# Starting the instruction streams of four engines at multiples of 128 slots in a one-token attention and MLP kernel

## The chip, the cores and the metric

The kernel runs on one core of one Trainium2 chip. The metric is the device time of one execution in microseconds (us); lower is better. Quoted times are medians of several executions. Beside them stands the span of one profiled execution, from its first to its last recorded instruction. The span is about 1.8 us shorter than the time of the same execution (659.0 and 660.86 us for the kernel before).

## The reference

Two sequences, one new token each, 32 heads of 128, a cache of 8192 positions, then a gated MLP. All inputs are bf16.

```python
def _A_ref(x, k_cache, v_cache, wq, wo):          # x: (2, 1, 512); caches: (2, 32, 8192, 128)
    q = (x @ wq).reshape(B, Sq, Hq, Dh).transpose(0, 2, 1, 3)
    scores = jnp.einsum("bhqd,bhkd->bhqk", q, k) * (Dh ** -0.5)
    p = _softmax(scores, axis=-1)
    o = jnp.einsum("bhqk,bhkd->bhqd", p, v)
    return o.transpose(0, 2, 1, 3).reshape(B, Sq, Hq * Dh) @ wo
# ... _B_ref: relu(x @ W_gate) * (x @ W_up) @ W_down
h = x + _A_ref(_layernorm(x), A_k_cache, A_v_cache, A_wq, A_wo)
h2 = h + _B_ref(_layernorm(h), B_W_gate, B_W_up, B_W_down)
```

The two caches are 268 MB of the 281.13 MB that the profile counts, so nearly all the traffic is one pass over K and V.

## The kernel before

The 64 pairs of sequence and head are worked off in 16 groups of four heads. One group is 8.4 MB of K and 8.4 MB of V. VectorE multiplies K by the query and adds up by halves, ScalarE takes exponentials, and TensorE multiplies by V. SyncE issues the loads. GpSimd builds constants in the first 8 us and is idle from then until about 634 us.

The kernel writes its own instruction lists, one for each engine, and emits them at the end (cut):

```python
class Streams:
    ...
    def emit(self, eng, engine):
        for waits, fn, gives in self.lists[eng]:
            for name, value in waits:
                engine.wait_ge(self.sem(name), value)
            if fn is not None:
                last = fn()
                if gives is not None and last is not None:
                    last.then_inc(self.sem(gives[0]), gives[1])
```

The first entries are these (cut). On ScalarE and SyncE the first entries are loads:

```python
    s.op("pool", lambda: pool.memset(eps_t, EPS), writes=["eps"])
    # ... mean_c, ident
    s.op("pool", lambda: pool.affine_select(out=ident, ...), reads=["ident"], writes=["ident"])
    s.op("pool", lambda: pool.memset(row_of, 0.0), writes=["row_of"])
    # ...
    s.dma("act", "dx", lambda: act.dma_start(out=x_row, ...), writes=["x_row"])
    s.dma("sp", "dwq", lambda: sync.dma_start(out=wq_v, ...), writes=["va", "vb", "vc"])
    load_k(0, 0, T // 2)
    load_k(0, T // 2, T)
    load_k(1)
    # ... from here on the layer norm, the query, the loop
    for n in range(L):                       # L = 15 of the 16 groups
        # ...
        scores(n, HALVES if n == 0 else (0, T))   # VectorE, then ScalarE
        if n + 2 < N:
            load_k(n + 2)
        # ...
```

The softmax here doesn't subtract the row's maximum and nothing guards it: scores larger than these inputs give would overflow.

Of the kernel before, what the change touches and what calls it, by code (L numbers as in the profile page):

```python
# [17 lines left out]
class Streams:  # L18
# [65 lines left out]
    def dma(self, eng, name, fn, reads=(), writes=(), extra=()):  # L84
        return self.op(eng, fn, reads, writes, extra, (name, 16), (name, 16))

    def wait(self, eng, tokens):
        self.lists[eng].append((self.needs(eng, (), (), tokens), None, None))

# [3 lines that stand above are left out]
                engine.wait_ge(self.sem(name), value)  # L93
            if fn is not None:
                last = fn()
                if gives is not None and last is not None:
                    last.then_inc(self.sem(gives[0]), gives[1])


# [1 line left out]
def kernel(  # L101
# [109 lines left out]
    s = Streams(nc, ("pe", "dve", "act", "pool", "sp"))  # L211
    for name in ("v_in", "p_in", "o_in"):
        s.sem(name)
    pe, dve, act, pool, sync = nc.tensor, nc.vector, nc.scalar, nc.gpsimd, nc.sync



    s.op("pool", lambda: pool.memset(eps_t, EPS), writes=["eps"])
    s.op("pool", lambda: pool.memset(mean_c, 1.0 / D), writes=["mean"])
    s.op("pool", lambda: pool.memset(ident, 0.0), writes=["ident"])  # L220
    s.op("pool", lambda: pool.affine_select(
        out=ident, in_=ident, compare_op=ALU.not_equal, fill=1.0, base=0, pattern=[[-1, P]],
        channel_multiplier=1), reads=["ident"], writes=["ident"])
    s.op("pool", lambda: pool.memset(row_of, 0.0), writes=["row_of"])
    s.op("pool", lambda: pool.memset(zm, 0.0), writes=["zm"])
    s.op("pool", lambda: pool.memset(pm, 0.0), writes=["pm"])
# [28 lines left out]
    def rows_of(cache, n):  # L255
        b, i = divmod(n, NQ)
        return cache[b, G * i:G * i + G].rearrange("h s d -> (h s) d").rearrange(
            "(p t) d -> p t d", p=P)
# [3 lines left out]
    def parts(lo, hi):  # L262
        cuts = [c for c in KEYS if lo <= c < hi]
        return [KEYS[c] for c in cuts]

    def load_k(n, lo=0, hi=T):
        t = kt[n % 2]
        keys = [f"k{n % 2}{x}" for x in parts(lo, hi)]
        s.dma("sp", f"dk{n}_{lo}", lambda: sync.dma_start(
            out=t[:, lo:hi, :], in_=rows_of(A_k_cache, n)[:, lo:hi, :]), writes=keys)  # L270
# [14 lines left out]
    load_k(0, 0, T // 2)  # L285
    load_k(0, T // 2, T)
    load_k(1)



# [484 lines left out]
```

## Time and profile before

| kernel before | value |
|---|---|
| time, median of 3 | 661.48 us (661.25 to 661.62) |
| span of the profiled execution | 659.0 us |
| start of the first product with K | 22.86 us |
| last landing of a load | 654.82 us |

The page of the kernel before follows, cut to the head, the rows of VectorE (DVE) and DMA in its 40 slices, and the queues. In the slices a 9 means busy for 90% or more of the slice. A queue line has packets, MB and share of the time of 16 transfer engines.

```profile
span 659.0 us, 3129 instructions
...
DVE  1799999999999999999999999999999999999962
...
DMA  9999999999999999999999999999999999999996
...
q1 hardware_dynamic: 6648, 281.06, 98.9%
q8 instruction: 3, 0.05, 0.0%
q14 instruction: 2, 0.02, 0.0%
```

The transfers are busy throughout (q1 for 98.9% of the span), and VectorE nearly so (617.2 us, 94%). The lines of kind "instruction" I take for the engines' own programs arriving: fifteen jumps to a new block, added on one engine, raised the packets on q14 from two to 16 (`act_15`) and 17 (`pool_15`, both below). By the trace's records each packet on q8 is 16 KB, and each on q14 is 8 KB.

The table of stretches of the kernel before has these columns: stretch, its length, busy us and instruction count of each engine, granted TensorE clock, DMA share, GB/s.

```profile
22.90:401.00 378.10, 53.44 (x600) 22.39 (x600) 375.88 (x86) 27.76 (x75) 0.00 (x0) 0.56 1.00 434
401.00:595.00 194.00, 29.63 (x328) 12.30 (x328) 190.39 (x44) 15.94 (x44) 0.00 (x0) 0.57 1.00 433
```

VectorE is busy for 375.88 of 378.10 us in the first stretch. In the second it leaves 3.6 us idle while the transfers stay at 1.00.

The timeline of the kernel before shows three products with K in that second stretch. Its columns are start, length, engine, line, operation, and in brackets the idle time of the engine and what ended it.

```profile
440.45 17.22 DVE L374 TENSOR_TENSOR k<-k,qrep 128x32768 bf16<-128x32768 bf16 x1 [0.42 <-DMA k<-in_A_k_cache_dram]
479.15 17.23 DVE L374 TENSOR_TENSOR k<-k,qrep 128x32768 bf16<-128x32768 bf16 x1 [0.72 <-DMA k<-in_A_k_cache_dram]
517.86 17.23 DVE L374 TENSOR_TENSOR k<-k,qrep 128x32768 bf16<-128x32768 bf16 x1 [0.72 <-DMA k<-in_A_k_cache_dram]
```

Each waits for its K load, and the period is 38.7 us. Before 400 us the period is 37.9 us, which is what VectorE needs for one group. So VectorE sets the pace first and the transfers set it later.

The beginning and the end come from the chain of work that ended last (start, length, what):

```profile
1.43 21.41 DMA k<-in_A_k_cache_dram
...
22.86 8.70 DVE k L374
...
641.94 12.88 DMA k<-in_B_W_down_dram
654.82 0.14 issue
654.95 0.42 PE y L667 x16
655.37 0.03 issue
655.40 0.29 DVE sc L731
```

The K load that lands at 22.83 us starts VectorE. The last W_down load, landing at 654.82 us, starts the last matmuls. Store and closing barrier follow, 4.2 us from that landing to the end of the span.

### The profile page before, as it was taken

Reading aid. Unit: us, or ns where it says so; the run is one execution under the profiler, and the core shown is the slowest. Engines: PE = TensorE matmul, PEld = TensorE weight load, DVE = VectorE, ACT = ScalarE, POOL = GpSimd, SP = SyncE. Lnnn points to the kernel's source line nnn. Section 1 sums busy time; section 2 is a strip of 40 time slices with the busy share of each in tenths; the row PEclk is TensorE's granted clock in tenths of the full one; section 3 lists DMA queues with packets and bytes.
Section 4 is the critical chain, followed back from the end, with each engine's and each line's share of the span. In section 5 each row is a group of like instructions: output and inputs, shape, how many; then the busy total and the mean of one; then the engine's idle time right before and its main releaser. Section 6 shows DMA issues by size and latency. Waiting matters only on the chain.

```text
span 659.0 us, 3129 instructions
## 1 busy us (share of the span) xinstructions
PE 114.0 (17%) x1244; PEld 47.1 (7%) x1244; DVE 617.2 (94%) x180; ACT 59.4 (9%) x155; POOL 7.7 (1%) x29
## 2 busy tenths in 40 slices
PE   2100302103030110303012030300203030030364
PEld 1000100001010000101000010100101010010112
DVE  1799999999999999999999999999999999999962
ACT  2301010010101001010100101010010101001100
POOL 3000000000000000000000000000000000000010
PEclk9755655657555575755557575555757555575776
DMA  9999999999999999999999999999999999999996
GB/s 382 443 445 434 398 442 445 445 434 398 442 445 442 442 398 442 442 445 438 430 410 442 445 442 434 402 445 442 442 442 402 438 442 442 442 426 414 432 411 244
DMA packets 6669, 281.13 MB, mean 427 GB/s; under 512 B 812, under 2 KB 816, under 8 KB 1544
## 3 DMA queue, kind: packets, MB, share of 16 engines
q1 hardware_dynamic: 6648, 281.06, 98.9%
q8 instruction: 3, 0.05, 0.0%
q14 instruction: 2, 0.02, 0.0%
q10 hardware_dynamic: 16, 0.01, 0.0%
HBM read 281.06 MB, written 0.00 MB: 426 GB/s over the span
## 4 chain that ended last, share of the span: by engine, by line
DVE 74%; DMA 24%; SPq 1%; issue 1%; PE 0%
DVE k L374 34%; DVE k L380 33%; DMA k<-in_A_k_cache_dram 22%; DVE sc L229 5%; DMA k<-in_B_W_down_dram 2%; SPq L549 1%; DVE osb L463 1%; DVE om L459 1%; SPq L540 0%; PE y L667 0%; SPq L283 0%; DVE ou L229 0%; DVE sc L731 0%; DVE rep L475 0%; SPq L770 0%
## 5 line engine op out<-in xcount | busy, mean ns | idle before, releaser
L374 DVE TENSOR_TENSOR k<-k,qrep 128x32768 bf16<-128x32768 bf16 (+3 forms) x18 | 275.9, 15327 | 4.9 <-DMA k<-in_A_k_cache_dram 4.9
L380 DVE TENSOR_TENSOR k<-k 128x4096 bf16<-128x4096 bf16 (+6 forms) x72 | 267.4, 3713 | 2.5
L416 PE MATMUL o<-v,pm 128*32 128x512 bf16 x960 | 85.8, 536 | 465.6 <-PEq L444 465.6
L393 ACT ACTIVATE pm<-sc 32x256 bf16<-32x256 f32 (+2 forms) x68 | 48.2, 709 | 563.1 <-DVE sc L229 562.3
L416 PEld LDWEIGHTS o<-v,pm 128*32 128x32 bf16 x960 | 36.1, 129 | 514.9 <-issue 508.6
L229 DVE TENSOR_REDUCE sc<-k 128x256 f32<-128x2048 bf16 (+2 forms) x17 | 36.7, 2161 | 0.6
L463 DVE TENSOR_REDUCE osb<-om 128x128 f32<-128x512 f32 x16 | 16.5, 1030 | 0.6
L393 ACT ACTIVATION_READ_ACCUMULATOR pm<-sc 32x1 f32 x68 | 15.8, 233 | 0.0
L359 DVE CAST qrep<-mm 32x512 bf16<-32x512 f32 x4 | 2.8, 695 | 11.5 <-PE mm L343 11.5
L459 DVE TENSOR_TENSOR om<-o,turn_of 128x512 f32<-128x512 f32 x16 | 10.9, 682 | 1.4 <-PE o L416 1.4
L423 PE MATMUL rep<-osb,spread 128*32 128x128 f32 x40 | 3.2, 363 | 47.7 <-DVE osb L463 44.5
L416 PE MATMUL o<-k,pm 128*32 128x512 bf16 x64 | 6.8, 583 | 8.7 <-ACT pm L393 5.8
L356 ACT ACTIVATE qrep<-mm 32x512 bf16<-32x512 f32 x12 | 7.0, 586 | 8.8 <-PE mm L343 8.5
L532 POOL TENSOR_TENSOR zm<-zm,zx 128x1 f32<-128x1 f32 x1 | 0.2, 190 | 626.2 <-ACT pm L393 626.2
L343 PE MATMUL mm<-v,om 128*64 128x512 bf16 x32 | 5.8, 512 | 9.3 <-DMA v<-in_A_wq_dram 8.4
L633 DVE STREAM_TRANSPOSE osb<-mm 128x512 f32<-128x512 f32 x1 | 0.7, 717 | 5.6 <-PE mm L617 5.6
L423 PEld LDWEIGHTS rep<-osb,spread 128*32 128x32 f32 x40 | 1.2, 127 | 50.0 <-DVE osb L463 46.1
L617 PE MATMUL mm<-v 128*2 128x512 bf16 x32 | 4.1, 609 | 0.9 <-DMA v<-in_A_wo_dram 0.8
L343 PEld LDWEIGHTS mm<-v,om 128*64 128x64 bf16 x32 | 2.3, 141 | 12.4 <-issue 9.7
L416 PEld LDWEIGHTS o<-k,pm 128*32 128x32 bf16 x64 | 2.0, 134 | 13.4 <-ACT pm L393 7.2
L731 DVE CAST sc<-y 128x128 bf16<-128x128 f32 x1 | 0.3, 291 | 2.7 <-PE y L667 2.7
L311 DVE COPY xc<-st 128x8 f32<-128x8 f32 x1 | 0.2, 166 | 2.7 <-PE st L304 2.7
(82 smaller groups left out, 35.1 us busy)
## 6 DMA issues: line engine op xcount, KB each, us to landing
k<-in_A_k_cache_dram SPq DMA_DIRECT2D x2, 4096.0 KB, 26.8
v<-in_A_wq_dram SPq DMA_DIRECT2D x1, 4096.0 KB, 12.2
k<-in_A_v_cache_dram SPq DMA_DIRECT2D x1, 4096.0 KB, 31.4
k<-in_A_v_cache_dram SPq DMA_DIRECT2D x1, 3072.0 KB, 38.3
v<-in_A_wo_dram SPq DMA_DIRECT2D x1, 2048.0 KB, 18.9
k<-in_B_W_gate_dram SPq DMA_DIRECT2D x1, 1376.0 KB, 14.8
k<-in_B_W_up_dram SPq DMA_DIRECT2D x1, 1032.0 KB, 17.0
k<-in_A_v_cache_dram SPq DMA_DIRECT2D x1, 1024.0 KB, 40.3
```

The costliest lines, as they stand in the source:

```text
L229: s.op("dve", lambda: dve.tensor_reduce(out=out_, in_=in_, axis=axis, op=ALU.add), reads=reads, writes=writes)
L343: last = pe.matmul(out=ps[h * B * Q:(h + 1) * B * Q], lhsT=xnb[:, c].rearrange("p b q -> p (b q)"), rhs=wq_h[:, c, g:g + QP, h0 + h, :], s ...
L356: s.op("act", lambda src=src, dst=dst: act.activation(out=dst, in_=src, func=ACT.Copy), reads=[f"mm{t}"], writes=[key])
L374: s.op("dve", lambda: dve.tensor_tensor(out=kp, in0=kp, in1=_view(qrep[:, b, i, :], 0, [[0, hi - lo], [1, Dh]]), op=ALU.mult), reads=keys ...
L380: s.op("dve", lambda half=half, width=width: dve.tensor_tensor(out=kp[:, :, 0:half], in0=kp[:, :, 0:half], in1=kp[:, :, half:width], op=AL ...
L393: last = act.activation(out=p_of[ps, lo // TG:hi // TG, :, h], in_=sc2[n % 2][ps, lo:hi].rearrange("p (g t) -> p g t", t=TG), func=ACT.Exp ...
L416: last = pe.matmul(out=o[g:g + W2], lhsT=pm[:, t // TG, :], rhs=vs[:, t:t + TG, :].rearrange("p t d -> p (t d)"), start=(t < P // Q * TG), ...
L423: return pe.matmul(out=rep_ps[u * Q:(u + 1) * Q, :], lhsT=spread.rearrange("k h m -> k (h m)"), rhs=osb[:, u, :], start=True, stop=True, s ...
L459: s.op("dve", lambda: dve.tensor_tensor(out=om.rearrange("p (t d) -> p t d", d=Dh), in0=o.rearrange("p (t d) -> p t d", d=Dh), in1=_view(t ...
L463: fn = lambda: dve.tensor_reduce(out=osb[:, u, :], in_=om.rearrange("p (t d) -> p d t", d=Dh), axis=AXIS.X, op=ALU.add)
L549: s.dma("sp", "d" + key, lambda: sync.dma_start(out=wd_sb[rows, f0:f0 + FT, :].rearrange("p j n -> p (j n)"), in_=wd_in[q0:min(q1, NM):row ...
L617: last = pe.matmul(out=ar_ps[g:g + B], lhsT=oc[:, k, :], rhs=wo_sb[:, k, :], start=False, stop=(k + P // Q >= NK), skip_group_check=True)
```

## The change

The intent, as I read it, is that an engine should not cross from one block of its program to the next at an awkward place. By a block I mean what one 8 KB instruction packet brings; that a multiple of 128 slots is the edge of one was not measured. The directive `addr_align(128, ...)`, put behind each engine's first instructions, asks that the stream go on at the next multiple of 128 instruction slots. The trace of after shows one branch more on each of the four engines (3133 instructions instead of 3129): VectorE's at 0.97 us, ahead of its first instruction, ScalarE's at 1.51 us, after its first load, GpSimd's at 1.66 us, after building the identity, and SyncE's at 2.94 us, after its four first loads. TensorE is left as it is.

```diff
+    def new_block(self, eng, engine):
+
+        self.lists[eng].append(((), lambda: engine.addr_align(128, offset=0, max_nops=0), None))
+
@@ emit
-                if gives is not None and last is not None:
+                if gives is not None:
@@
+    s.new_block("dve", dve)
     s.op("pool", lambda: pool.memset(eps_t, EPS), writes=["eps"])
@@
         channel_multiplier=1), reads=["ident"], writes=["ident"])
+    s.new_block("pool", pool)
@@
     load_k(1)
+    s.new_block("sp", sync)
+    s.new_block("act", act)
```

The changed line in `emit` drops a test and adds no work. The diff adds 8 lines ahead of the loop, so L374 is L382.

## The prediction

Three passages are cut out of the recorded text where it is marked, since no trace or run of this case shows them: a statement on how instructions are fetched, an estimated cost of a jump whose target had not been fetched yet, and a count of where the second crossings lie. 661.2 us is the 661.48 us of before less a gain of about 0.3 us ("part of a microsecond"), with the branches off the critical path. "The shared queue" is q14 of the page.

> **What bounds the kernel now.** The data transfers, with VectorE close behind. 281 MB move at a mean of 427 GB/s over a 659.0 us span (page). In the stage table the stretch 22.9 to 401 us has DMA share 1.00 with VectorE busy 375.9 of 378.1 us; 401 to 595 us has DMA share 1.00 with VectorE busy 190.4 of 194.0 us. The period of a head group in the timeline is 37.9 us early and 38.7 us late, where VectorE waits for K loads. VectorE's start is set by the K landing at 22.83 us, the end by the last W_down landing at 654.8 us, then 4.2 us of matmul, copy, store and closing barrier.
>
> **What the change does.** The instruction order shows one extra directive on each of four engines and nothing moved. Each takes one branch over padding, so the rest of its stream starts at a multiple of 128 slots. This can only buy better placed crossings from one instruction block to the next. [...]
>
> **Gains and costs.** Inside the span of before there are two 8 KB instruction packets, at 177.2 and 201.3 us, 0.31 us each; one more starts at 659.4 us, behind the last instruction. Around 177 and 201 us there is no gap: VectorE goes on within 0.03 us, ScalarE had nothing to do. Near the likely second crossings[...] no gap lacks a semaphore that explains it. So the gain is at most part of a microsecond, in or behind the closing barrier.
>
> Cost: about 0.15 us a branch (those at 0.8 us)[...]. All jumps are early and off the critical path: SyncE's comes after its four loads are issued (2.9 us), its next issue at 20.05 us; VectorE waits for TensorE until 2.65 us; GpSimd's results are due at about 23 us. The normalised x is ready at 5.9 us, its consumer waits for wq until 13.25 us: 7 us of slack. The K landing at 22.8 us stays.
>
> **Predicted time: 661.2 us, range 659.8 to 662.6.** Chances: faster by over 2% 0.01, within 2% 0.98, slower by over 2% 0.01.
>
> **What would show it.** Right: first K product at 22.8 to 22.9 us; SyncE's first issues unchanged; the shared queue's instruction packets within the first few us instead of at 177 and 201, without a gap; periods 37.9 then 38.7 us; last landing within 0.5 us of 654.8. Wrong: a gap of 1 to 3 us in VectorE or SyncE without a semaphore to explain it, the first product after 23.5 us, or a tail off 4.2 us by over 0.5 us.
>
> **What would make it wrong.** A crossing in the tail of before whose fetch waits behind the data; a target that isn't fetched ahead; or a fetch block other than I think, so that the new layout crosses in the tail where the old one didn't.

## The result, and the profile after

| | before | after |
|---|---|---|
| time, median of 4 | 661.37 us (660.96 to 661.62) | 661.50 us (661.41 to 661.79) |
| span of the profiled execution | 659.0 us | 659.6 us |
| first product with K | 22.86 us | 23.60 us |
| last landing | 654.82 us | 655.72 us |
| last landing to end of span | 4.2 us | 3.9 us |

The ratio is 1.0003, with a 95% interval of 0.9986 to 1.0021. A ratio is the mean time of one kernel's runs over that of the other's runs of the same rounds, so it is not quite the ratio of the medians quoted here.

The page of the kernel after, the same lines:

```profile
span 659.6 us, 3133 instructions
...
DVE  1799999999999999999999999999999999999962
...
DMA  9999999999999999999999999999999999999995
...
q1 hardware_dynamic: 6648, 281.06, 98.8%
q8 instruction: 3, 0.05, 0.0%
q14 instruction: 6, 0.05, 0.0%
```

The data is the same, but there are six instruction packets of 8 KB in the span instead of two.

The table of stretches of the kernel after:

```profile
22.90:401.00 378.10, 55.01 (x600) 22.84 (x600) 375.17 (x85) 27.37 (x74) 0.00 (x0) 0.56 1.00 434
401.00:595.00 194.00, 29.40 (x328) 12.24 (x328) 191.04 (x45) 16.47 (x45) 0.00 (x0) 0.57 1.00 433
```

The regime is unchanged.

Beginning and end of the chain of work of the kernel after:

```profile
1.44 22.14 DMA k<-in_A_k_cache_dram
...
23.60 8.70 DVE k L382
...
642.82 12.90 DMA k<-in_B_W_down_dram
655.72 0.14 issue
655.86 0.42 PE y L675 x16
656.28 0.02 issue
656.30 0.29 DVE sc L739
```

The first K load lands 0.7 us later although it was issued at the same time. The last landing is 0.9 us later.

The products with K in the second stretch, timeline of the kernel after:

```profile
440.69 17.22 DVE L382 TENSOR_TENSOR k<-k,qrep 128x32768 bf16<-128x32768 bf16 x1
479.00 17.23 DVE L382 TENSOR_TENSOR k<-k,qrep 128x32768 bf16<-128x32768 bf16 x1 [0.34 <-DMA k<-in_A_k_cache_dram]
518.06 17.23 DVE L382 TENSOR_TENSOR k<-k,qrep 128x32768 bf16<-128x32768 bf16 x1 [1.08 <-DMA k<-in_A_k_cache_dram]
```

By 479 us the 0.7 us lost at the start have been given back, because here the loads set the pace and not VectorE. The wait at 518.06 us is 0.36 us longer than the same wait of before.

Two things are not on the page and come from the trace's records. The first is the start of each 8 KB instruction packet:

| | 8 KB instruction packets, start in us |
|---|---|
| before | 177.2, 201.3 (and 659.4, behind the span) |
| after | 4.1, 6.5, 6.6, 7.4, 482.7, 509.1 |

The second is the closing barrier. After its first wait there (658.22 us in before, 659.13 us in after), VectorE's next instruction starts 0.49 us later in before and 0.11 us later in after. ScalarE's and SyncE's follow after 0.09 us in both. VectorE's next step is what the others then wait for, so the change shortens the end by 0.3 to 0.4 us.

So there is a cost at the start, a gain at the end, and a later last landing. All are under 1 us, which the runs' scatter could also produce. The experiments ask which of these differences is real.

### The profile page after: what moved, and what is told of

The parts are those of the page before. It is cut to its first block, busy times and chain, and to the rows that moved or that the text cites. A ratio compares the mean times of both kernels' runs of the same rounds, so it can differ in the third digit from the quotient of the medians. Undisturbed runs are those within 1.5% of the kernel's fastest.

```text
span 659.6 us, 3133 instructions
## 1 busy us (share of the span) xinstructions
PE 116.0 (18%) x1244; PEld 47.7 (7%) x1244; DVE 617.1 (94%) x180; ACT 59.4 (9%) x155; POOL 7.9 (1%) x29
## 4 chain that ended last, share of the span: by engine, by line
DVE 79%; DMA 18%; SPq 1%; issue 1%; PE 0%
DVE k L382 36%; DVE k L388 36%; DMA k<-in_A_k_cache_dram 16%; DVE sc L235 5%; DMA k<-in_B_W_down_dram 2%; DVE osb L471 1%; SPq L557 1%; DVE om L467 1%; SPq L548 0%; DVE ou L235 0%; DVE rep L483 0%; PE y L675 0%; SPq L289 0%; DVE sc L739 0%; SPq L778 0%
## 5 line engine op out<-in xcount | busy, mean ns | idle before, releaser
L382 DVE TENSOR_TENSOR k<-k,qrep 128x32768 bf16<-128x32768 bf16 (+3 forms) x18 | 275.9, 15327 | 4.5 <-DMA k<-in_A_k_cache_dram 4.5
L424 PE MATMUL o<-v,pm 128*32 128x512 bf16 x960 | 87.7, 545 | 462.6 <-PEq L452 462.6
```

What stands on the lines that cost most here:

```text
L382: s.op("dve", lambda: dve.tensor_tensor(out=kp, in0=kp, in1=_view(qrep[:, b, i, :], 0, [[0, hi - lo], [1, Dh]]), op=ALU.mult), reads=keys ...
L424: last = pe.matmul(out=o[g:g + W2], lhsT=pm[:, t // TG, :], rhs=vs[:, t:t + TG, :].rearrange("p t d -> p (t d)"), start=(t < P // Q * TG), ...
```

## The experiments

**Theory A.** The differences are real. By this theory, instruction packets travel on the transfer engines that also carry K and V, and a packet puts the one engine that carries it behind the other 15. A load has landed when its slowest engine has, so the delay would show in every later load. VectorE's 0.5 us in the closing barrier of before would be its crossing into a new block.

**Rival B.** Two executions of one kernel differ by that much, and the packets are absorbed. **A2** is a weaker form of A, in which a packet costs only its own 0.31 us.

The two traces agree with the premise of A. Each large load leaves 16 landing events, which I take for one from each of the 16 transfer engines. The first product with K starts right after the last of the 16 of its load: 22.83 and 22.86 us in before, 23.58 and 23.60 us in after. For wq the events are spread from 12.65 to 13.14 us in before and from 12.71 to 13.88 us in after. Only the last events moved, so most transfer engines were as fast as before and at least one was 0.7 us late.

The results of all runs, in the order of the sections below. "Packets" counts 8 KB instruction packets inside the span. "Period" is the mean of four late periods, taken from the starts of the products with K. "Step" is VectorE's step in the closing barrier. Times in us.

| run | time, median | ratio to before (95%) | packets | first K product | period | last landing | step | span |
|---|---|---|---|---|---|---|---|---|
| first profile of before | | | 2 | 22.86 | 38.70 | 654.82 | 0.49 | 659.05 |
| first profile of after | | | 6 | 23.60 | 38.70 | 655.72 | 0.11 | 659.61 |
| before_again | 661.28 | 1.0002 (0.9988 to 1.0016) | 2 | 22.91 | 38.70 | 654.65 | 0.49 | 658.88 |
| after_again | 661.52 | 1.0006 (0.9992 to 1.0019) | 6 | 23.88 | 38.69 | 655.98 | 0.11 | 659.88 |
| dve_only | 661.43 | 1.0004 (0.9990 to 1.0017) | 3 | 23.68 | 38.74 | 655.98 | 0.11 | 660.08 |
| no_dve | 661.36 | 1.0004 (0.9990 to 1.0017) | 5 | 23.58 | 38.62 | 655.38 | 0.49 | 659.79 |
| act_15 | 670.24 | 1.0136 (1.0120 to 1.0151) | 16 | 22.86 | 39.39 | 664.32 | 0.49 | 668.55 |
| pool_15 | 669.98 | 1.0128 (1.0113 to 1.0144) | 17 | 22.87 | 39.36 | 664.21 | 0.49 | 668.64 |
| pool_marks | 661.03 | 0.9997 (0.9982 to 1.0012) | 3 | 23.02 | 38.70 | 654.95 | 0.49 | 659.38 |
| both_15 | 671.49 | 1.0160 (1.0144 to 1.0175) | 31 | 22.85 | 39.48 | 664.82 | 0.49 | 669.22 |
| dve_5_slots | 661.37 | 0.9998 (0.9985 to 1.0012) | 3 | 23.00 | 38.70 | 655.54 | 0.11 | 659.63 |
| dve_3_slots | 661.13 | 0.9998 (0.9985 to 1.0012) | 3 | 23.01 | 38.71 | 655.42 | 0.11 | 659.31 |
| dve_1_slot | 660.93 | 1.0000 (0.9986 to 1.0013) | 3 | 23.05 | 38.70 | 654.89 | 0.12 | 658.77 |
| dve_2_slots | 661.05 | 1.0001 (0.9987 to 1.0014) | 3 | 22.83 | 38.70 | 654.77 | 0.11 | 658.66 |

The 9 runs of before beside each group had medians of 661.19 us (before_again to no_dve), 661.44 us (act_15 to pool_marks, and dve_5_slots), 661.11 us (both_15, dve_3_slots) and 661.12 us (dve_1_slot, dve_2_slots). All runs gave correct results. `act_15`, `pool_15` and `both_15` are apart from before, since their intervals exclude 1.

### Both kernels once more, and the jumps taken apart

`before_again` and `after_again` are the two kernels unchanged. `dve_only` keeps one jump of the change:

```diff
     s.new_block("dve", dve)
-    s.new_block("pool", pool)
-    s.new_block("sp", sync)
-    s.new_block("act", act)
```

`no_dve` keeps the other three:

```diff
-    s.new_block("dve", dve)
     s.new_block("pool", pool)
     s.new_block("sp", sync)
     s.new_block("act", act)
```

before_again:

> The unchanged kernel once more, to see what a second profile of it repeats. Theory A (the early instruction packets cost, the closing barrier gains): first K product again at 22.8 to 22.9 us, two 8 KB instruction packets of the shared queue inside the span near 177 and 201 us, VectorE's last two steps of the closing barrier again about 0.5 us apart (658.225 to 658.719 us in the first profile), 661.4 us. Rival B (both differences are scatter between executions): first K product anywhere in 22.8 to 23.6 us and the 0.5 us step not repeated.

after_again:

> The changed kernel once more. Theory A: first K product again at 23.5 to 23.7 us, four 8 KB packets at 4 to 8 us and two at about 480 and 510 us, VectorE's last barrier step about 0.1 us instead of 0.5 us, 661.5 us, ratio to before 0.999 to 1.001. Rival B: first K product as likely at 22.9 us, the barrier step varies.

dve_only:

> The jump on VectorE alone. Theory A: one 8 KB packet in the first 10 us instead of four, so the first K product is at 22.8 to 23.1 us; VectorE's barrier step is 0.1 us as in the changed kernel; time 0.2 to 0.5 us under before, about 661.0 us. Rival B: no difference from before beyond scatter.

no_dve:

> The jumps on ScalarE, GpSimd and SyncE, none on VectorE. Theory A: three 8 KB packets in the first 10 us, first K product at 23.2 to 23.6 us, VectorE's packet again near 201 us, its barrier step 0.5 us as in before; time 0.2 to 0.8 us over before, about 661.8 us. Rival B: no difference from before beyond scatter.

Measured: the differences repeat. The first product with K started at 22.91 us without early packets and at 23.58 to 23.88 us with them (`after_again`, at 23.88 us, lies a little above what A gave). In these four runs and the two first profiles, VectorE's step in the barrier is 0.11 us where VectorE jumps and 0.49 us where it does not. Rival B falls for both.

One expectation of A was wrong. `dve_only` has a single early packet, at 4.1 us, and its first product is as late (23.68 us) as with four packets (23.60 us) or three (23.58 us). So early packets do not add up. That fits if each engine's program comes over a transfer engine of its own: four of the 16 are late by one packet each, and the load is late by one. The 16 landings of wq agree. In the runs without early packets the latest of them came at 13.31 us. Later than that were one landing in `dve_only` (13.94 us), three in `no_dve` (13.39, 13.59, 13.82 us), four in `after_again` (13.42 to 14.13 us), and three in after (13.65 to 13.88 us) with a fourth at 13.31 us. `both_15` below tests it again.

The runs also name the packets. `dve_only` has packets at 4.1, 199.1 and 483.0 us, `no_dve` at 6.5, 6.6, 7.5, 179.4 and 509.3 us. So VectorE owns the one near 177 us in before and those at 4.1 and 483 us in after, and ScalarE owns those near 201 and 509 us (in `act_15` below, where ScalarE jumps elsewhere, the one near 201 us is gone). The expectation for `no_dve` had VectorE's packet near 201 us and was wrong there.

The times do not separate these kernels. The medians of the three kernels with jumps lie 0.2 to 0.3 us over before's, and every interval contains 1; `no_dve`, expected near 661.8 us, came out at 661.36 us. The expected 661.0 us for `dve_only` was not seen, because its last landing came 1.2 us later than before's. What it gained in the barrier it had lost already. Its end was also 0.2 us slower for a reason outside the change: from the last landing to VectorE's last cast it took 0.78 us, against 0.58 us in before and after. The same 0.2 us shows in `no_dve`, `pool_marks` and `dve_5_slots`, whether VectorE jumps or not.

### Fifteen jumps instead of one

If a packet costs anything, many packets must show it. Starting from before, `act_15` makes ScalarE jump once after each group of the loop. ScalarE is busy for only about 4 us of each 38 us period.

```diff
         if n + 2 < N:
             load_k(n + 2)
+        s.new_block("act", act)
```

`pool_15` does it on GpSimd, which is otherwise idle then. It first clears one value at the end of each group, so that the jumps are spread as ScalarE's are:

```diff
         if n + 2 < N:
             load_k(n + 2)
+        s.op("pool", lambda: pool.memset(warm, 0.0), writes=["warm"],
+             extra=[s.last[f"sc{n % 2}"]])
+        s.new_block("pool", pool)
```

`pool_marks` is the control: the clearings without the jumps.

act_15:

> Before, with ScalarE (busy about 4 us of each 38 us period) jumping to a new block once after each of the 15 head groups in the loop: about 15 packets of 8 KB in the span instead of ScalarE's one. Theory A (one packet puts the one transfer engine that carries it 0.6 to 0.8 us behind the other 15, that stays, and each transfer lands with its slowest engine): the last of the 16 landings of a load falls ever further behind the first, from 1.8 us to about 10 us at the end, and the time rises by 6 to 10 us, to 667 to 671 us. Theory A2 (the packet costs its bytes alone, 0.31 us): plus 2 to 4 us. Rival B (fetches are absorbed, first products merely scatter): within 0.5 us of before.

pool_15:

> Before, with GpSimd (idle from 8 to 634 us) clearing one value and jumping to a new block after each of the 15 head groups: about 15 packets of 8 KB. Theory A: plus 6 to 10 us as for ScalarE's 15. Theory A2: plus 2 to 4 us. Rival B: within 0.5 us of before.

pool_marks:

> The control: the same 15 clearings on GpSimd without the jumps, no added packets beyond at most one or two for the longer stream. All theories: within 0.5 us of before. If it slows as the one with the jumps does, the clearings and not the packets cost.

Measured: plus 8.8 and 8.5 us on the medians, and nothing for the control. The clearings do not cost, and it does not matter which engine jumps. Both results lie in the range that A gave and outside those of A2 and B.

The products with K of `act_15` in the timeline:

```profile
445.68 17.22 DVE L377 TENSOR_TENSOR k<-k,qrep 128x32768 bf16<-128x32768 bf16 x1 [1.42 <-DMA k<-in_A_k_cache_dram]
485.07 17.22 DVE L377 TENSOR_TENSOR k<-k,qrep 128x32768 bf16<-128x32768 bf16 x1 [1.40 <-DMA k<-in_A_k_cache_dram]
524.45 17.23 DVE L377 TENSOR_TENSOR k<-k,qrep 128x32768 bf16<-128x32768 bf16 x1 [1.41 <-DMA k<-in_A_k_cache_dram]
```

Where before waits 0.72 us for a K load, this run waits 1.40 us. The period is 39.39 us instead of 38.70, so one packet per period costs 0.69 us per period. The landings say the same. For the V load that lands at 624.30 us in before, the first of the 16 landings came at 622.53 us and the last 1.77 us later. In `act_15` the first came at 622.28 us and the last 10.77 us later. That is 9.0 us more, and it is one landing alone: the other 15 had come by 623.99 us (623.62 us in before). `pool_15` has the same picture, one landing at 632.52 us and 15 by 624.33 us. A load issued late, because of the pause of an engine that jumps, is a poor explanation for one landing that moves alone. One transfer engine out of 16 is late.

The trace also shows why a packet of 0.31 us costs 0.69 us. In this part of the program a data packet of 64 KB takes 2.42 us (median), and each transfer engine runs one directly after the other. A packet of `act_15` at 368.83 us begins within 4 ns of the end of such a data packet and takes 0.309 us. The data packet that begins at its end takes 2.796 us, 0.38 us more than usual. The sum is 0.68 us, and all 15 of ScalarE's packets in this run give 0.67 to 0.71 us. GpSimd's 15 in `pool_15` give 0.66 to 0.67 us, and its period is 39.36 us. VectorE's packets cost more: the one at 482.7 us in after takes 0.332 us and the data packet behind it 3.080 us, 0.99 us in all; over all runs VectorE's in the loop gave 0.84 to 1.04 us. Why the next data packet is longer, and why by more behind VectorE's, is not shown. What the trace does show is an instruction packet slipped in between two whole data packets; what decides on that order is not shown either.

Not every packet is paid for. In `pool_15` the starts of the products are those of before until 288 us (within 0.1 us), and only then does the period rise to 39.4 us. My reading is that the lagging transfer engine has time in hand while VectorE sets the pace.

### Both loads of jumps at once

`both_15` has the jumps of `act_15` and of `pool_15` together.

> Both of the loads of 15 jumps at once: ScalarE's and GpSimd's, 30 packets of 8 KB in the span. If each engine's packets go over a transfer engine of its own, the slowest of 16 is as late as with one of the two: about 670 us, late periods 39.4 us, as each alone had. If they share one transfer engine, it is twice as late: late periods about 40.1 us and 680 us or more.

Measured: 671.49 us and a period of 39.48 us, about as with one of the two and far from 680 us. The packets of the two engines therefore do not queue on one transfer engine. The landings of the same V load show it: two of the 16 are late, at 633.41 and 633.97 us, and the other 14 came by 624.40 us. The period is 0.09 us longer than in `act_15`, and the packets fit that: where one of each engine run within 0.6 us of each other, each costs its transfer engine 0.74 to 0.80 us.

The packet records support it. I followed the 64 KB data packets from end to next start, which gives 16 chains; in after, each has exactly 240 such packets. Along these chains all 15 packets of GpSimd's jumps in `pool_15` lie on one chain. In after, VectorE's two packets lie on one, ScalarE's two on another, and GpSimd's and SyncE's on two more. Steps between chains are ambiguous in some places (in `act_15` and `both_15` the label changes on the way), so this supports the landings and is no proof alone.

### Moving VectorE's crossing by a few slots

Can the gain at the end be had without the packet at the start? These kernels take before and put empty instructions ahead of VectorE's list, to bring the old crossing a few slots earlier. There is no jump.

```diff
+    for _ in range(5):                      # 3, 2 or 1 in the other runs
+        s.lists["dve"].append(((), lambda: dve.engine_nop(), None))
     s.op("pool", lambda: pool.memset(eps_t, EPS), writes=["eps"])
```

dve_5_slots:

> Before, with five empty instructions in front of VectorE's first instruction, no jump: VectorE's crossing that I place in the closing barrier moves five slots earlier, into a wait for TensorE's last product. Theory A: no packet in the first 10 us, first K product at 22.8 to 22.9 us as in before; barrier step of VectorE 0.1 us instead of 0.5 us; the last landing as in before (654.6 to 654.9 us); span 0.3 to 0.4 us under before's, time about 660.9 us. Rival B: the barrier step stays 0.5 us or the last landing moves anyway.

dve_3_slots:

> As the five empty instructions, but three, so that VectorE's crossing falls behind its last copy, where it waits anyway, and its packet (1 to 3 us later) behind the last W_down landing. Theory A: last landing back at 654.6 to 654.9 us (655.5 us with five), packet at 656 to 658 us, barrier step 0.1 us, span 658.5 to 658.7 us, time 0.2 to 0.5 us under before. Rival: the packet meets the store of the output and gives the gain back, span 658.9 us or more; or the step of 0.5 us is back.

dve_1_slot:

> One empty instruction instead of three or five. With three the packet still ran at 654.2 us, before the last landing, so VectorE's sequencer reaches the crossing while its last copy waits. With one, the crossing should fall between the second drain of the closing barrier (656.5 us) and the wait that ends at 658.2 us, which hides it: packet at 657.5 to 659 us, last landing at 654.6 to 654.9 us as in before, barrier step 0.1 us, span 658.5 to 658.7 us; time 0.2 to 0.5 us under before. Rival: no better than before, because the packet delays the store's landing or the step stays 0.5 us.

dve_2_slots:

> Two empty instructions. Either as with one (packet after 656.5 us, last landing 654.6 to 654.9 us, span 658.5 to 658.7 us) or, if the sequencer fetches two slots ahead, as with three (packet at 654.2 us, last landing 655.4 us, span 659.3 us).

Measured, with five: the step in the barrier is 0.11 us as hoped, but the packet that follows the crossing now runs at 654.3 us, and the last landing is at 655.54 us instead of 654.65 to 654.82 us. The expectation had counted a moved landing for Rival B. What speaks for A is that again one landing moved alone: of the eight landing events of the last W_down load, seven came by 654.44 us (654.36 us in before). With three, the packet still ran at 654.2 us and the last landing was 655.42 us; the expectation of A for this run was wrong, because the crossing is reached earlier than I had placed it.

With one and with two, the packet ran at 657.8 and 657.7 us, behind the last landing (654.89 and 654.77 us). The waits inside the barrier hide the crossing. In `dve_2_slots` it can be seen there: VectorE's drain ahead of that wait starts 0.39 us after TensorE's and takes 0.33 us, where in every other run it starts within 0.1 us of TensorE's and takes 0.01 us. The spans are the shortest, 658.77 and 658.66 us against 659.05 and 658.88 us of before. The medians, 660.93 and 661.05 us against 661.12 us, do not separate them from before (0.2 to 0.5 us less had been expected for `dve_1_slot`): ratios 1.0000 and 1.0001, with intervals 0.27% wide. So no version is shown to beat either kernel. What is shown is that the barrier step moves with the slot count.

## Why the prediction was right or wrong

**Right: the time and the bound.** 661.2 us was forecast and 661.5 us measured. The kernel is limited by its transfers, as said. `act_15` is the strongest evidence: 0.69 us per period added on one transfer engine arrived in the time of the kernel. That the number came within 0.3 us is in part luck: a gain of 0.3 to 0.4 us at the end and a later last landing, which the prediction did not have, work against each other.

**Wrong: "All jumps are early and off the critical path", so "The K landing at 22.8 us stays."** The waits of the four instruction streams did have slack, and that was all I had looked at. I had overlooked that a jump also orders a packet (`dve_only`: one jump, one early packet at 4.1 us), and that the packet goes over a transfer engine that carries wq and K (one landing of wq alone at 13.94 us there, the others by 13.31 us). The first product came at 23.60 and 23.88 us instead of 22.8 to 22.9, past the 23.5 us that the prediction itself had named as a sign that it was wrong. That failed step did not move the time, because the second half of the kernel, where the loads set the pace, gave those 0.7 us back by 479 us.

**Wrong: "last landing within 0.5 us of 654.8".** It was 655.72 and 655.98 us. In `after`, `dve_only` and `no_dve`, VectorE or ScalarE has fetched twice before the tail, and the last landing came 0.6 to 1.2 us later than in the first profile of before. In `pool_marks`, `dve_1_slot` and `dve_2_slots` none of the four engines has fetched twice by then, and it stayed within 0.13 us. With a second packet of VectorE at 654.2 to 654.3 us (`dve_5_slots`, `dve_3_slots`) it came 0.6 to 0.7 us later. This roughly fits the cost of a packet, 0.69 us for ScalarE's at 509 us and 0.99 us for VectorE's at 483 us. One transfer engine sets the end: in `dve_only` seven of the eight landing events of the last W_down load came by 654.63 us and the last at 655.98 us, against 654.36 and 654.82 us in before. That it is the engine that carries VectorE's or ScalarE's program is argued, not shown, because I could not follow the chains of packets through the small loads of the tail.

**Half right: the instruction packets.** I expected them in the first microseconds instead of at 177 and 201 us. Four came there, and two more at 482.7 and 509.1 us. So the change has six packets in the span where before has two.

**Too small: "about 0.15 us a branch".** ScalarE's first table load moved from 1.51 to 1.96 us (1.97 us in `no_dve`, 1.52 us in `dve_only`), so its jump cost 0.45 us. GpSimd's next clearing moved only from 2.05 to 2.12 us. None of this was on the critical path.

**Right in kind, missed in before: "part of a microsecond, in or behind the closing barrier".** The gain is 0.38 us in VectorE's step, which the removal of its jump (`no_dve`) undoes. I had written that no gap in the tail of before lacked a semaphore to explain it. That step is such a gap, seen when VectorE is set beside ScalarE at the same wait.

In sum, the gain of 0.3 to 0.4 us at the end is real. In the profiled executions it is more than spent by a last landing 0.9 to 1.2 us later (after and `after_again`), and the net, 0.1 to 0.3 us on the medians, is below what the intervals resolve.

## What to carry to other kernels

In this kernel, which keeps all transfer engines full (DMA share 1.00 from 22.9 to 595 us), instruction fetches are traffic. A jump into a new block cost two things here: a pause of the engine that jumps (0.45 us on ScalarE, 0.07 us on GpSimd), and 0.66 to 1.04 us (packets in the loop) on one of the 16 transfer engines, which later loads inherited. Where VectorE set the pace it cost no time (`pool_15` until 288 us); where the loads set it, it did (0.69 us per period in `act_15`). Before placing code at block boundaries, look for packets of kind "instruction" and for the spread of a load's 16 landings. Where an engine must cross a block, try to let it cross while it waits anyway and after the last load that matters has landed: with one and two slots the step was 0.12 and 0.11 us instead of 0.49 us and the last landing stayed at 654.89 and 654.77 us, though the medians did not separate these runs from before.
